# Two of five held chunks become late ones, two sums move one stretch ahead, and a block of the second stage goes first

## The chip, the cores and the metric

The kernel runs on one core of one Trainium2 chip, in float32 throughout. The metric is the device time in microseconds (us) of one execution, median of three runs.

## What is computed

For each of 8 sequences `x` (6400 steps, 128 channels) the kernel computes a causal convolution with a filter `h` as long as the sequence, and then a gated layer on its result:

```
y    = irfft(rfft(x, 2S) * rfft(h, 2S))[:S]          # per channel
gate = sigmoid(sum over k of conv_w[k] * y[t - 4 + k])   # 5 taps, causal
out  = (gate * (y @ w_val)) @ w_out
```

## The kernel before, in words

**Stages.** The transforms are written as matrix products. A sequence is laid out as 100 x 64 (`N1` x `N2`). The **first stage** (`Forward`) takes sums and differences of two halves of `x` (`sums`: one subtraction on GpSimd, POOL in the profile, and one addition, on POOL too inside the main loop) into one of three buffers `sd_0..2`, and multiplies them on TensorE, PE (`half`, 16 small products into two PSUM banks); two copies on ScalarE, ACT, bring the result into `gy`. 16 such blocks make a sequence. The **second stage** (`Product`, 13 blocks `kb`) multiplies `gy` with the constants `m2` on PE; VectorE, DVE, multiplies the result with the filter's spectrum (`mul_u`, `mul_t`), and POOL makes sums of that (`add`), back into `gy`. The constants and the spectrum of each block, 512 KB each, are loaded anew by the queue on SyncE (SP) into slices of one buffer, `ring` (`m2_sb`, `h_sb`). The **third stage** (`s3_quads`, 16 groups) goes from `gy` to `dt`: 64 products on PE, two copies on ACT (`keep`, `ends`) and two joins on DVE (`join`). The **fourth stage** (`s4`) makes the convolved `y` in 13 chunks of 5 (the head: 4) of the 64 columns.

**A chunk's work after `s4`.** ACT copies `y` out of PSUM (`copies`). ACT starts the next columns' gate sums (`init`), and puts the product of one tap into a scratch (`keep`, buffers `keeps`); DVE adds three taps (`taps`, `more`, scalar_tensor_tensor); POOL adds the scratch (`add`). Then PE multiplies `y` with `w_val` (`project`), ACT takes the sigmoid (`sigm`), DVE multiplies (`gate`), PE multiplies with `w_out` (`output`), ACT copies, and SP stores (`store`). Every engine's order is the order of the program text (`_InOrder`), so a waiting instruction holds all that stands behind it on its engine.

**Two stretches per sequence.** In the *third-stage stretch* of sequence b (line 616, group g = 0 to 15) each group holds: third stage of b, one first-stage block of b + 1 with the `sums` for the block two further on, and what `steps[g]` lists: deferred chunk work of b - 1. In the *mixed stretch* (line 665, step s = 0 to 14) stand the fourth stage of b and the second stage of b + 1. So the second stage of b + 1 shares a stretch with the fourth of b, and its products go into `gy` before the next third stage begins.

**Which work is deferred.** `HELD` and `LATE` split the chunks by their first column `a`. Chunks below 10 are done within the mixed stretch. *Held* chunks (10, 15, 20, 25, 30) do their taps and adds in the mixed stretch; projection, gate, output and store wait for groups 0 to 7 of the third-stage stretch. *Late* chunks (35 to 55) have only `y` copied in the mixed stretch; their taps stand two and one groups ahead of their projection. In the mixed stretch the order is head, 0, late ones, 5, held ones, so the held chunks' taps and adds stand at its very end.

**Buffers around the change.** `keeps` has four scratches: two slices of `sd_0` and `sd_1`, and `p_0`, `p_1`. Four single PSUM banks (`single`) go around among `s4`, `half`, `project` and `output`; two pairs (`pair`) among second and third stage. Held gate sums and held `y` lie in `ring`, where `m2_load` and `h_load` of the next sequence may only write once they are out (`AHEAD`). Chunk 5's output is copied into `dt` and stored from there, so the joins of group 0, which write `dt`, wait for that store.

**Where the first two `sums` stand before.** Lines 613 to 615: ahead of group 0, behind the last held chunk's `add` (the `sd` buffers serve as scratches until then). The three loads of `x` they need are issued at step 10 (line 706).

Names in the profile: helpers record every instruction, so all lines read L111; a tile says which work it is: `sd<-x` sums, `pt<-r_sb,sd` first-stage products, `pt<-r_sb,gy` third-stage products, `pt<-gy,ring` second-stage products, `pt<-m_sb,dt` fourth-stage products, `dt<-pt,ring` joins, `gy<-pt,ring` and `ring<-pt,ring 128x1024` the multiplications with the spectrum, SCALAR_TENSOR_TENSOR taps, `pt<-ring,w_sb` and `pt<-yl,w_sb` projections and outputs.

Of the kernel before, what the change touches and what calls it, by code (L numbers as in the profile page):

```python
# [17 lines left out]
N1 = 100  # L18
# [12 lines left out]
CH = 5  # L31
HEAD = (60, 4)
# [2 lines left out]
OUT_ORDER = CHUNKS[1:] + [HEAD]  # L35
LATE = 35
HELD = 10
BL = 2 * SB * C
M2B = 3
MH = 6  # L40
HB = 4
XB = 3
# [81 lines left out]
def longconv_moe(ctx: ExitStack, tc: tile.TileContext, x, h, r1, m2, r3, m4, w64, out):  # L124
    nc = _Engines(tc)
    B = x.shape[0]
# [24 lines left out]
    h_sb = [ring_at[M2B + i] for i in (2, 0, 1, 3)]  # L151
    held_c = ring[:, : (LATE - HELD) * N1].rearrange("p (n t) -> p n t", t=N1)
    held_y = {
        a: ring[:, i : i + CH * N1].rearrange("p (n t) -> p n t", t=N1)
        for a, i in zip(range(HELD, LATE, CH), (2500, 3072, 3572, 4096, 4596))
    }
    x_sb = [cp.tile([128, 2, XG, N2], F32, name=f"x_{i}") for i in range(XB)]
    sd_sb = [cp.tile([128, 2, XG, N2], F32, name=f"sd_{i}") for i in range(3)]
    p_t = [cp.tile([128, CH, N1], F32, name=f"p_{i}") for i in range(2)]
    keeps = [t.rearrange("p a d n -> p (a d n)")[:, : CH * N1].rearrange("p (n t) -> p n t", t=N1) for t in sd_sb[:2]] + p_t  # L160
    hd = dp.tile([NKB, 128, 2 * SB * C], F32, name="hd")

    def weights():
# [66 lines left out]
    def single():  # L230
        return ps1.tile([128, 512], F32, name="pt1", tag="pt1")
# [171 lines left out]
    def cells(x, n):  # L403

        out, i = [], 0
        while i < n:
            y = x + i
            end = next(e for e in (4, HELD, LATE, N2) if y < e)
            k = min(n - i, end - y)
            s = (y - 4) % N2  # L410
            t, o = (gl, y - LATE) if y >= LATE else (held_c, y - HELD) if y >= HELD else (dv[:, :, 1, :N1], s)
            out.append((i, t[:, o : o + k]))
# [3 lines left out]
    class Chunk:  # L416


        def __init__(self, b, i, ch, defer):
            self.b, self.i, self.ch = b, i, ch  # L420
            a, n = ch
            self.late = defer and LATE <= a < HEAD[0]
            self.held = defer and HELD <= a < LATE
            self.y = yl[a][:, :n] if a >= LATE else held_y[a] if a >= HELD else dv[:, a : a + n, 0, :N1]

        def s4(self):
# [39 lines left out]
                self.p = self.y  # L466

        def keep(self):
            self.q = p_t[self.i % 2] if self.late else keeps[self.i % 4]
            self.first(3, self.q, self.p)  # L470

        def init(self):
# [71 lines left out]
    fh, fx = Forward(h, gh, xh), Forward(x[0], gy, xh, NS)  # L544
# [44 lines left out]
    fx = Forward(x[1], gy) if B > 1 else None  # L589
    if fx:  # L590
        fx.load(XB)
    pend = []
    for b in range(B):
        nxt = b + 1 < B


        steps = collections.defaultdict(list)
        for c in pend:
            a = c.ch[0]
            if a == HEAD[0]:  # L600
                t = NS - 1
            elif c.held:
                t = (a - HELD) // CH
            else:
                t = 6 + 2 * (a - LATE) // CH
                steps[t - 2] += [lambda c=c: c.taps(range(2))]
                steps[t - 1] += [lambda c=c: c.taps(range(2, 4)), c.add]
            steps[t] += [c.project, c.sigm, c.gate]
            if t + 2 < NS:
                steps[t + 2] += [c.output]  # L610
                steps[t + 3] += [c.store]
        pend = [c for c in pend if c.ch[0] in (HEAD[0], HEAD[0] - CH)]
        if nxt:
            for _ in range(2):
                fx.sums(nc.gpsimd)
        for g in range(NS):
            e = s3_quads(4 * g)
            f = []
            if nxt:
                f = fx.half([single(), single()])  # L620
                fx.sums(nc.gpsimd)
            for u in e:
                u()
            for u in f:
                u(act)
            if b == 0:
                next(wgen, None)
                next(wgen, None)
                if g % 3 == 0 and g < 12:
                    m4_load(m4_rest.pop(0))  # L630
            if nxt and g in AHEAD:
                f, kb = AHEAD[g]
                (h_load if f else m2_load)(kb)
            for u in steps[g]:
                u()
        if nxt:
            h_load(HB - 1)
        if b + 2 < B:
            fx = Forward(x[b + 2], gy)


        chs = CHUNKS if not nxt else sorted(CHUNKS, key=lambda c: (c != HEAD, c[0] > 0, c[0] < LATE))
        cs = [Chunk(b, i, ch, nxt) for i, ch in enumerate(chs)]
        jobs = collections.defaultdict(list)
        for i, c in enumerate(cs):
            if i and not c.late and not c.held:
                jobs[i + 3].append(c)
        if not nxt:
            jobs[NCH + 2].append(cs[0])
        pr = {}  # L650

        def s2(kb):
            if nxt and kb < NKB:
                pr[kb] = Product(kb)
                m2_load(kb + M2B)

        def times(kb):
            if kb in pr:
                pr[kb].mul_u()
                pr[kb].mul_t()  # L660
                pr.pop(kb).add()
                h_load(kb + HB)

        outs, at = [], 0
        for s in range(max(NCH, *jobs) + 2):
            kbs = list(range(at, min(at + 2 - s % 2, NKB))) if nxt else []
            at += len(kbs)
            if s < 2:
                cs[s].s4()
            late = pend[s : s + 1]  # L670
            if late and s == 0:
                late[0].output()
                late[0].store(p_t[1][:, : HEAD[1]])
                late = []
            if s == 0:
                s2(0)
            for kb in kbs[:1]:
                s2(kb + 1)
            if m4_rest:
                m4_load(m4_rest.pop(0))  # L680
            for c in jobs[s]:
                c.project()
            if 1 < s < NCH:
                cs[s].s4()
            for c in outs + late:
                c.output()
            for c in jobs[s]:
                c.sigm()
            for kb in kbs[:1]:
                times(kb)  # L690
            for kb in kbs[1:]:
                s2(kb + 1)
            if s < NCH:
                cs[s].copies()
            for c in outs + late:
                c.store()
            for kb in kbs[1:]:
                times(kb)
            if 0 < s <= NCH and not cs[s - 1].late:
                cs[s - 1].taps()  # L700
            if 2 < s < NCH + 2 and not cs[s - 2].late:
                cs[s - 2].add()
            for c in jobs[s]:
                c.gate()
            outs = jobs[s]
            if s == 10 and b + 2 < B:
                fx.load(XB)
        pend = [cs[0]] + [c for c in cs if c.held or c.late]


# [43 lines left out]
```

## Time and profile before

| | us |
|---|---|
| three runs, median (lowest to highest) | 1033.85 (1031.86 to 1035.61) |
| profiled execution, its own time | 1034.45 |
| its span | 1032.6 |
| PE busy | 874.2 (85%) |
| DVE busy | 744.7 (72%) |
| POOL busy | 563.4 (55%) |
| ACT busy | 505.1 (49%) |

The granted TensorE clock is 0.953 of full speed in the mean. After a setup the two stretches alternate: the first group of a third-stage stretch starts its first-stage products at 215.24, 337.15, 456.64, 580.04, 699.62 and 818.78 us, so one sequence takes some 120.7 us. The seventh and last third-stage stretch has no next sequence, and no first-stage work.

How to read it: a busy share is a mean over stretches with different limits. A timeline row gives start, length, engine, operation, tiles, count, and in brackets the idle time ahead of it with what ended it. "issue" is idle time for which the profile shows no cause.

### The profile page before, as it was taken

The page shows a single profiled execution, that of the slowest core. Times are in us where ns is not written, and L with a number is a line of the kernel's source. Part 1 is how long each engine was busy: PE and PEld are TensorE (multiplying, and loading weights), DVE is VectorE, ACT ScalarE, POOL GpSimd, SP SyncE. Part 2 cuts the span into 40 slices and gives each one's busy share as a digit, 9 for nine tenths or more (in the row PEclk, how much of TensorE's full clock was granted, in tenths as well). Part 3 has the DMA queues.
Part 4 walks back from the last instruction along what each step waited for, and adds up shares of the span by engine and source line. Part 5 has one row for each costly group of instructions (what it writes and reads, how often), then busy time and mean ns, then how long its engine had stood idle before and what let it go on. Part 6 is the DMA issues. An engine that isn't in the chain of part 4 may idle for free.

```text
span 1032.6 us, 47904 instructions
## 1 busy us (share of the span) xinstructions
PE 874.2 (85%) x21360; PEld 700.7 (68%) x21360; DVE 744.7 (72%) x1049; ACT 505.1 (49%) x1215; POOL 563.4 (55%) x594
## 2 busy tenths in 40 slices
PE   6798679978897979969899698978899698999698
PEld 6798668845696558945588466965579465885464
DVE  5456649758588587867687586984878676888786
ACT  4431542447424673247624484245732575246476
POOL 5457527665386554865357653855648653672122
PEclk9799989989999899989899899998999898999999
DMA  7684649436492466715485355824667154831112
GB/s 245 224 299 182 204 140 329 158 114 187 130 315 75 135 198 210 258 53 165 135 280 180 93 169 167 306 88 129 202 202 268 53 157 149 292 131 53 53 50 98
DMA packets 76364, 177.40 MB, mean 172 GB/s; under 512 B 17792, under 2 KB 29312, under 8 KB 76160
## 3 DMA queue, kind: packets, MB, share of 16 engines
q1 hardware_dynamic: 76160, 174.35, 51.0%
q8 instruction: 168, 2.75, 1.1%
q14 instruction: 36, 0.29, 0.1%
HBM read 141.56 MB, written 32.77 MB: 169 GB/s over the span
## 4 chain that ended last, share of the span: by engine, by line
PE 54%; DVE 12%; issue 9%; ACT 5%; POOL 3%; DMA 1%; DVEq 0%; SPq 0%; ACTq 0%; POOLq 0%
PE pt L111 54%; DVE ring L111 5%; DVE dt L111 4%; DVE gy L111 2%; ACT ring L111 2%; DVE gl L111 2%; DMA ring<-m 1%; POOL gl L111 1%; ACT gl L111 1%; ACT p L111 1%; POOL sd L111 1%; ACT dt L111 1%; POOL ring L111 1%; POOL gy L111 0%; ACT sd L111 0%
## 5 line engine op out<-in xcount | busy, mean ns | idle before, releaser
L111 POOL TENSOR_TENSOR gy<-gy,ring 128x512 f32<-128x512 f32 (+1 forms) x182 | 220.2, 1242 | 122.5 <-DVE ring L111 77.2
L111 PEld LDWEIGHTS pt<-r_sb,gy 64*64 64x64 f32 x8192 | 148.8, 142 | 113.2 <-issue 81.9
L111 POOL TENSOR_TENSOR sd<-x 128x256 f32<-128x256 f32 x236 | 175.4, 770 | 79.7 <-issue 55.3
L111 DVE TENSOR_TENSOR dt<-pt,ring 128x496 f32<-128x496 f32 x256 | 160.1, 667 | 78.7 <-ACT dt L111 78.3
L111 PEld LDWEIGHTS pt<-m_sb,dt 128*64 128x64 f32 x4096 | 185.2, 136 | 39.8 <-issue 11.8
L111 PE MATMUL pt<-r_sb,sd 50*64 50x100 f32 x4608 | 150.9, 270 | 72.2 <-POOL sd L111 42.9
L111 PE MATMUL pt<-m_sb,dt 128*64 128x100 f32 x4096 | 193.8, 249 | 14.5 <-DVE dt L111 6.7
L111 PE MATMUL pt<-r_sb,gy 64*64 64x64 f32 x8192 | 166.2, 230 | 41.4 <-issue 30.0
L111 ACT COPY ring<-pt 128x512 f32<-128x512 f32 (+2 forms) x216 | 129.4, 603 | 145.0 <-PE pt L111 86.7
L111 PE MATMUL pt<-gy,ring 128*64 128x128 f32 x3008 | 188.5, 278 | 12.8 <-PE pt L111 10.3
L111 PEld LDWEIGHTS pt<-gy,ring 128*64 128x64 f32 x3008 | 176.0, 135 | 21.6 <-PE pt L111 17.9
L111 PEld LDWEIGHTS pt<-r_sb,sd 50*64 50x64 f32 x4608 | 126.5, 149 | 79.7 <-POOL sd L111 44.3
L111 DVE TENSOR_TENSOR ring<-pt,ring 128x1024 f32<-128x1024 f32 (+2 forms) x131 | 134.8, 1029 | 51.8 <-PE pt L111 41.4
L111 DVE TENSOR_TENSOR gy<-pt,ring 128x1024 f32<-128x1024 f32 (+1 forms) x99 | 116.8, 1180 | 67.3 <-PE pt L111 63.7
L111 ACT COPY gy<-pt 128x400 f32<-128x400 f32 x248 | 111.3, 504 | 77.8 <-PE pt L111 76.8
L111 POOL TENSOR_TENSOR gl<-gl,p 128x500 f32<-128x500 f32 (+1 forms) x38 | 47.1, 1238 | 143.5 <-DVE gl L111 111.9
L111 ACT COPY dt<-pt 128x16 f32<-128x16 f32 (+3 forms) x317 | 67.4, 265 | 105.0 <-PE pt L111 104.9
L111 ACT COPY yl<-pt 128x500 f32<-128x500 f32 (+1 forms) x89 | 51.1, 574 | 125.0 <-PE pt L111 124.9
L111 DVE SCALAR_TENSOR_TENSOR ring<-pt,w_sb,ring 128x500 f32<-128x500 f32 (+4 forms) x136 | 91.8, 675 | 9.0 <-ACT sd L111 1.7
L111 DVE SCALAR_TENSOR_TENSOR gl<-yl,w_sb,gl 128x500 f32<-128x500 f32 (+1 forms) x112 | 95.6, 858 | 2.8 <-POOL sd L111 1.4
L111 PE MATMUL pt<-ring,w_sb 128*64 128x500 f32 x320 | 84.9, 632 | 1.5 <-DVE ring L111 1.4
L111 DVE TENSOR_TENSOR gl<-pt,gl 128x500 f32<-128x500 f32 (+1 forms) x48 | 31.6, 660 | 34.9 <-ACT gl L111 18.3
(54 smaller groups left out, 751.2 us busy)
## 6 DMA issues: line engine op xcount, KB each, us to landing
ring<-m SPq DMA_DIRECT2D x90, 512.0 KB, 5.2
ring<-hd SPq DMA_DIRECT2D x84, 512.0 KB, 4.7
x<-xl SPq DMA_DIRECT2D x118, 256.0 KB, 3.0
out<-ring SPq DMA_DIRECT2D x40, 250.0 KB, 2.7
out<-yl SPq DMA_DIRECT2D x40, 250.0 KB, 2.7
m_sb<-m SPq DMA_DIRECT2D x12, 375.0 KB, 5.9
hd<-ring SPq DMA_DIRECT2D x8, 512.0 KB, 5.0
out<-dt SPq DMA_DIRECT2D x16, 250.0 KB, 3.8
```

The costliest lines, as they stand in the source:

```text
L111: return self._tc.keep_in_program_order(call(*args, **kwargs))
```

## The change

`WAIT = 25` splits the held chunks: 10, 15 and 20 stay held, 25 and 30 become late ones, with `init`, `keep`, `taps` and `add` in groups 0 to 3 of the third-stage stretch, ahead of their projections, which stay where they were. These taps now read `y` from `ring` instead of PSUM. The scratches no longer use `sd_0` and `sd_1`, but `p_0`, `p_1` and two halves of `h_sb[0]`. That frees `sd_0` and `sd_1`, and the first two `sums` move from the head of the third-stage stretch to steps 9 and 10 of the mixed stretch ahead; the loads of `x` move from step 10 to step 5. Last, the first block of the second stage, `s2(0)`, is issued ahead of the head chunk's `s4`, not behind it.

```diff
+WAIT = 25
...
-    keeps = [t.rearrange("p a d n -> p (a d n)")[:, : CH * N1].rearrange("p (n t) -> p n t", t=N1) for t in sd_sb[:2]] + p_t
+    keeps = p_t + [h_sb[0][:, i : i + CH * N1].rearrange("p (n t) -> p n t", t=N1) for i in (0, BL // 2)]
...
-            self.late = defer and LATE <= a < HEAD[0]
-            self.held = defer and HELD <= a < LATE
+            self.late = defer and WAIT <= a < HEAD[0]
+            self.held = defer and HELD <= a < WAIT
...
-            self.q = p_t[self.i % 2] if self.late else keeps[self.i % 4]
+            self.q = p_t[self.i % 2] if self.late else keeps[(self.i + self.i // 8) % 4]
...
         fx.load(XB)
+        for _ in range(2):
+            fx.sums(nc.gpsimd)
...
-                t = 6 + 2 * (a - LATE) // CH
-                steps[t - 2] += [lambda c=c: c.taps(range(2))]
-                steps[t - 1] += [lambda c=c: c.taps(range(2, 4)), c.add]
+                k = (a - WAIT) // CH
+                t = max(3 + k, 2 + 2 * k)
+                steps[2 * k] += [lambda c=c: c.taps(range(2))]
+                steps[2 * k + 1] += [lambda c=c: c.taps(range(2, 4)), c.add]
...
-        if nxt:
-            for _ in range(2):
-                fx.sums(nc.gpsimd)
...
+            if s == 0:
+                s2(0)
             if s < 2:
                 cs[s].s4()
...
-            if s == 0:
-                s2(0)
...
-            if s == 10 and b + 2 < B:
-                fx.load(XB)
+            if b + 2 < B:
+                if s == 5:
+                    fx.load(XB)
+                if s in (9, 10):
+                    fx.sums(nc.gpsimd)
```

**POOL, end of the mixed stretch and start of the third-stage stretch**, before: the last second-stage `add`, then the chunks' adds (their target is `dt`, `ring` or `gl`), then the sums.

```order
L111 TENSOR_TENSOR gy<-gy,ring 128x64x4 x2
L111 TENSOR_TENSOR dt<-dt,p_88 128x2x100
L111 TENSOR_TENSOR ring<-ring,p_88 128x300
L111 TENSOR_TENSOR ring<-ring,sd_84 128x500
L111 TENSOR_TENSOR ring<-ring,sd_85 128x500
L111 TENSOR_TENSOR ring<-ring,p_87 128x500
L111 TENSOR_TENSOR ring<-ring,p_88 128x500
L111 TENSOR_TENSOR ring<-ring,sd_84 128x200
L111 TENSOR_TENSOR gl<-gl,sd_84 128x300
L111 TENSOR_TENSOR sd_84<-x_81 128x256 x2
L111 TENSOR_TENSOR sd_85<-x_82 128x256 x2
L111 TENSOR_TENSOR sd_86<-x_83 128x256 x2
```

The same place now (a scratch in `h_sb[0]` shows as `ring`):

```order
L112 TENSOR_TENSOR gy<-gy,ring 128x64x4 x2
L112 TENSOR_TENSOR dt<-dt,ring 128x2x100
L112 TENSOR_TENSOR ring<-ring 128x300
L112 TENSOR_TENSOR sd_84<-x_81 128x256 x2
L112 TENSOR_TENSOR ring<-ring,p_88 128x500
L112 TENSOR_TENSOR sd_85<-x_82 128x256 x2
L112 TENSOR_TENSOR ring<-ring 128x500 x2
L112 TENSOR_TENSOR sd_86<-x_83 128x256 x2
L112 TENSOR_TENSOR sd_84<-x_81 128x256 x2
L112 TENSOR_TENSOR ring<-ring,p_88 128x500
L112 TENSOR_TENSOR sd_85<-x_82 128x256 x2
```

The first two pairs of sums now stand behind the adds of chunks 5 and 10; chunk 25's add stands behind two further pairs, inside group 1.

**DVE at the same border**, before: taps of chunk 30, then the joins of group 0 (`dt<-pt,ring`), a gate (`ring<-pt,ring`), the next joins.

```order
L111 SCALAR_TENSOR_TENSOR ring<-pt_2955,w_sb,ring 128x500
L111 SCALAR_TENSOR_TENSOR ring<-pt_2955,w_sb,ring 128x400
L111 SCALAR_TENSOR_TENSOR gl<-pt_2955,w_sb,gl 128x100
L111 SCALAR_TENSOR_TENSOR ring<-pt_2955,w_sb,ring 128x300
L111 SCALAR_TENSOR_TENSOR gl<-pt_2955,w_sb,gl 128x200
L111 TENSOR_TENSOR dt<-pt_2998,ring 128x124x4
L111 TENSOR_TENSOR dt<-pt_2998,ring 128x62x2x4
L111 TENSOR_TENSOR ring<-pt_3059,ring 128x500
L111 TENSOR_TENSOR dt<-pt_3064,ring 128x124x4
L111 TENSOR_TENSOR dt<-pt_3064,ring 128x62x2x4
L111 TENSOR_TENSOR ring<-pt_3125,ring 128x500
```

Now, from the taps of chunk 20 on:

```order
L112 SCALAR_TENSOR_TENSOR ring<-pt_2895,w_sb,ring 128x500 x3
L112 TENSOR_TENSOR dt<-pt_2982,ring 128x124x4
L112 TENSOR_TENSOR dt<-pt_2982,ring 128x62x2x4
L112 TENSOR_TENSOR ring<-pt_3043,ring 128x500
L112 SCALAR_TENSOR_TENSOR ring<-ring,w_sb 128x500 x2
L112 TENSOR_TENSOR dt<-pt_3052,ring 128x124x4
L112 TENSOR_TENSOR dt<-pt_3052,ring 128x62x2x4
L112 TENSOR_TENSOR ring<-pt_3113,ring 128x500
L112 SCALAR_TENSOR_TENSOR ring<-ring,w_sb 128x500
L112 TENSOR_TENSOR dt<-pt_3120,ring 128x124x4
L112 TENSOR_TENSOR dt<-pt_3120,ring 128x62x2x4
```

The joins of group 0 follow chunk 20's taps, and chunk 25's taps stand behind the gates of groups 0 and 1; chunk 30's follow in groups 2 and 3.

**PE at the border the other way**, from the third-stage into the mixed stretch, before: the head chunk's projection for sequence b - 1, the head chunk's `s4` for b, the head chunk's output for b - 1, and the first two blocks of the second stage for b + 1.

```order
L111 MATMUL pt_4095<-yl_74,w_sb 64x400 x2
L111 MATMUL pt_4103<-m_sb,dt 64x2x50 x16
L111 MATMUL pt_4120<-gl,w_sb 64x400 x2
L111 MATMUL pt_4125<-gy,ring 64x64x2 x16
L111 MATMUL pt_4143<-gy,ring 64x64x2 x16
```

Now:

```order
L112 MATMUL pt_4095<-yl_74,w_sb 64x400 x2
L112 MATMUL pt_4103<-gy,ring 64x64x2 x16
L112 MATMUL pt_4121<-m_sb,dt 64x2x50 x16
L112 MATMUL pt_4138<-gl,w_sb 64x400 x2
L112 MATMUL pt_4143<-gy,ring 64x64x2 x16
```

The first second-stage block has changed places with `s4` and the output. On SP, two loads of `x` that each wait for one of the moved pairs of sums now stand ahead of chunk 5's store from `dt`; before they stood behind it.

## The prediction

> **What bounds the kernel now.** I read the page first. PE is the busiest engine and heads the chain that ended last, so what PE waits for comes next.
>
> ```profile
> PE 54%; DVE 12%; issue 9%; ACT 5%; POOL 3%; DMA 1%; DVEq 0%; SPq 0%; ACTq 0%; POOLq 0%
> ```
>
> The waits: one PE wait is long and rare, six times up to 7.2 us for the first-stage sums; the other has no cause in the profile.
>
> ```profile
> PE pt L111 <- issue: 50.8, 34, 4.2
> ...
> PE pt L111 <- POOL sd L111: 42.9, 6, 7.2
> ```
>
> Six is the number of third-stage stretches that carry first-stage work and follow a mixed stretch. PE's timeline at one of these borders (start, length, tiles, count):
>
> ```profile
> 448.30 1.19 PE L111 MATMUL pt<-r_sb,gy 64*64 64x64 f32 x64
> 456.64 1.61 PE L111 MATMUL pt<-r_sb,sd 50*64 50x100 f32 x32 [7.16 <-POOL sd L111]
> ...
> 461.57 0.86 PE L111 MATMUL pt<-r_sb,sd 50*64 50x100 f32 x32
> ...
> 463.36 1.19 PE L111 MATMUL pt<-r_sb,gy 64*64 64x64 f32 x64
> 464.37 0.87 PE L111 MATMUL pt<-r_sb,sd 50*64 50x100 f32 x32
> ...
> 467.00 1.19 PE L111 MATMUL pt<-r_sb,gy 64*64 64x64 f32 x64
> ```
>
> Group 0's third-stage products end at 449.5, and its first-stage block starts at 456.64. After the wait the same work also takes longer: 1.61 against 0.86 us for a block. The view by stretches says why: the granted clock (the third figure from the end) is 0.50 behind the wait, and 1.00 from the next block on.
>
> ```profile
> 456.70:460.00 3.30, 3.30 (x36) 1.54 (x36) 0.00 (x0) 1.41 (x3) 2.62 (x4) 0.50 0.50 153
> 461.60:467.00 5.40, 5.40 (x153) 3.02 (x143) 3.19 (x5) 4.15 (x12) 2.81 (x5) 1.00 0.51 162
> ```
>
> POOL in the time of the wait, in the order of its text:
>
> ```profile
> 452.53 1.24 POOL L111 TENSOR_TENSOR ring<-ring,p 128x500 f32<-128x500 f32 x1 [1.00 <-issue]
> 453.73 0.60 POOL L111 TENSOR_TENSOR ring<-ring,sd 128x200 f32<-128x200 f32 x1
> ...
> 455.19 4.14 POOL L111 TENSOR_TENSOR sd<-x 128x256 f32<-128x256 f32 x6
> ```
>
> The sums stand behind chunk 30's add (at 453.73 the first of its two pieces), and that behind chunk 30's taps on DVE, the second of these rows:
>
> ```profile
> 445.45 4.70 DVE L111 SCALAR_TENSOR_TENSOR ring<-pt,w_sb,ring 128x500 f32<-128x500 f32 x6
> ...
> 450.32 1.41 DVE L111 SCALAR_TENSOR_TENSOR ring<-pt,w_sb,ring 128x500 f32<-128x500 f32 x2 [0.17 <-ACT sd L111]
> ```
>
> **Part 1: the first sums move ahead.** The first pair of sums now stands behind chunk 5's add and the second behind chunk 10's, so neither waits for chunks 15 to 30. Chunk 20's taps are the first three of the six at 445.45, over at 447.8; chunk 10's lie ahead of 445.45. So both pairs are there before 449.5, and group 0's first-stage block can follow its third-stage products at once. Its first PSUM bank is chunk 20's, free at 447.8 as well. This removes the wait, 42.9 us in all, and the slow start behind it: block to block it is 461.57 - 456.64 = 4.93 us after the wait, 464.37 - 461.57 = 2.80 in the next group, which has the same projection and third-stage work. That is 2.13 us here; at another border
>
> ```profile
> 215.24 1.61 PE L111 MATMUL pt<-r_sb,sd 50*64 50x100 f32 x32 [7.15 <-POOL sd L111]
> ...
> 219.76 0.86 PE L111 MATMUL pt<-r_sb,sd 50*64 50x100 f32 x32
> ```
>
> it is 4.52 - 2.80 = 1.72. Taking 1.9, six times: 11.5 (10.3 to 12.8). Part 1 gains 42.9 + 11.5 = 54.4 us.
>
> The same slow start by a page: the Trainium skill, TensorE: Matmul & The Clock Gate, Part 1 (the HAM clock gate), halves PE's clock after an idle window of about 3.4 us until one such window of work has passed; an estimate by its figure is 1.7 us for each wait, 53.1 instead of 54.4 in all. By that rule the clock at 0.50 behind the wait is as it should be, and the rows differ from the estimate by 0.2 us a wait.
>
> What is late next? Group 0's joins on DVE. They follow chunk 20's taps, so DVE is free for them at 447.8 and their PSUM is ready about 450.1. But they write `dt`, so they wait for chunk 5's store out of it:
>
> ```profile
> 447.30 0.55 SPq L111 DMA_DIRECT2D out<-dt  x1
> ```
> ```profile
> out<-dt SPq DMA_DIRECT2D x16, 250.0 KB, 3.8
> ```
>
> On SP this store now stands behind a load of `x` that waits for the second pair of sums, which I place at some 447.7; so it issues at about 448.1, and lands at 451.9. The joins then end at 453.2, and PE's group 2, which needs their PSUM pair, comes about 454: just hidden, by 0.9 us.
>
> **Part 2: taps of chunks 25 and 30 move.** PE's work in each group is the same as before. On DVE about 5.2 us leave the mixed stretch, where it has no slack, for groups 0 to 3:
>
> ```profile
> L111 DVE TENSOR_TENSOR dt<-pt,ring 128x496 f32<-128x496 f32 x256 | 160.1, 667 | 78.7 <-ACT dt L111 78.3
> ...
> L111 DVE SCALAR_TENSOR_TENSOR gl<-yl,w_sb,gl 128x500 f32<-128x500 f32 x105 | 89.5, 852 | 2.8 <-POOL sd L111 1.4 <-ACT gl L111 0.2
> ...
> L111 DVE SCALAR_TENSOR_TENSOR ring<-pt,w_sb,ring 128x500 f32<-128x500 f32 x104 | 76.7, 738 | 8.7 <-ACT sd L111 1.7 <-ACT p L111 1.5 <-DVE ring L111 0.5
> ...
> L111 POOL TENSOR_TENSOR sd<-x 128x256 f32<-128x256 f32 x236 | 175.4, 770 | 79.7 <-issue 55.3 <-PE pt L111 13.6 <-DMA x<-hl 4.7
> ...
> L111 DVE TENSOR_TENSOR ring<-pt,ring 128x500 f32<-128x500 f32 x40 | 27.0, 676 | 45.3 <-PE pt L111 41.4 <-ACT ring L111 3.2
> ```
>
> Six taps at 852 ns, the price with `y` from SBUF (738 from PSUM), are 5.1; two are cut in two pieces, so 5.2. With eight joins at 667 (5.3) and four gates at 676 (2.7) DVE has 13.2 us to do in groups 0 to 3. PE needs 467.00 - 463.36 = 3.64 for a group with projection and output, 14.6 for four. So it fits, at 90%, with little room: a late gate or sigmoid then shows. The nearest row for such a chain is in the last stretch, where ACT waits for POOL's add:
>
> ```profile
> 963.35 0.62 ACT L111 ACTIVATE gl<-gl 128x500 f32<-128x500 f32 x1 [2.45 <-POOL gl L111]
> ```
>
> I bound what comes back by 0 and 2.5 us a sequence and take 1.0, nearer to nothing since PE hides most of it: 6 x 1.0 = 6.0. ACT's four moved activations and POOL's two adds stand in groups where those engines have idle time.
>
> The seventh stretch has no first-stage work, so DVE sets its pace already:
>
> ```profile
> 955.43 1.20 PE L111 MATMUL pt<-r_sb,gy 64*64 64x64 f32 x64 [0.95 <-DVE dt L111]
> ...
> 961.43 1.19 PE L111 MATMUL pt<-r_sb,gy 64*64 64x64 f32 x64 [0.79 <-DVE dt L111]
> ```
>
> There the 5.2 us are only moved, but the two new chains through ACT and POOL may add waits: 1.0 us (0 to 4).
>
> **Part 3: second stage's first block first.** At the other border:
>
> ```profile
> 391.83 0.89 PE L111 MATMUL pt<-yl,w_sb 128*64 128x400 f32 x4
> 393.51 1.69 PE L111 MATMUL pt<-m_sb,dt 128*64 128x100 f32 x31 [0.78 <-DVE dt L111]
> ...
> 395.66 4.00 PE L111 MATMUL pt<-gy,ring 128*64 128x128 f32 x64
> 400.43 2.07 PE L111 MATMUL pt<-gy,ring 128*64 128x128 f32 x32 [0.78 <-PE pt L111]
> ```
> ```profile
> 391.97 0.90 ACT L111 COPY gy<-pt 128x400 f32<-128x400 f32 x2
> ```
> ```profile
> 397.84 1.22 DVE L111 TENSOR_TENSOR gy<-pt,ring 128x1024 f32<-128x1024 f32 x1 [3.94 <-PE pt L111]
> ...
> 400.24 1.22 DVE L111 TENSOR_TENSOR gy<-pt,ring 128x1024 f32<-128x1024 f32 x1
> ```
>
> `s2(0)` needs only `gy`, complete at 392.9, where `s4` waited for the joins until 393.5. The four pieces to the end of `s2(1)` took 393.51 to 399.66; started at 392.9 they end at 399.1. DVE has then done block 0's two products and starts block 1's at 399.2 instead of 400.24. From there DVE runs without a gap and PE waits for it, so 1.0 us is gained at each of 7 borders: 7.0. It is 0 if PE sets the pace there, and 1.6 (both waits of 0.78) at most.
>
> **The sum.** 1034.45 - 54.4 - 7.0 + 6.0 + 1.0 = 980.05. The median of the runs lies 0.6 below the profiled execution: **979**. With all bounds on one side: 1034.45 - 55.7 - 11.2 - 0.6 = 967, and 1034.45 - 53.2 + 15 + 4 - 0.6 = 1000.
>
> **The rivals.**
>
> *DVE and POOL in each other's way (1008).* The moved taps read two SBUF operands while POOL makes sums. The Trainium skill, SBUF — State Buffer, "SBUF: two separate sides", speaks against the move: DVE with two SBUF inputs and a POOL operation exclude each other for a whole instruction. As a mechanism of this kernel: eight pieces, each held by one of POOL's sums (770 ns), are 6.2 us more, so DVE has 19.4 us in groups 0 to 3 against PE's 14.6; 4.8 us come back in six sequences, 979 + 29. For it: 852 against 738 ns. Against it: that is 0.11, not 0.77 a piece. 13%.
>
> *The first block still waits (1027).* If something else of group 0 or the chunks ahead ends as late as the sums did, only part 3 is left: 1034.45 - 7.0 - 0.6. The profile names no such wait: the PSUM bank and the adds ahead are free by 447.8. 6%.
>
> *Slower: PE starves for instructions (1050).* PE waits 50.8 us with no cause in the profile, in pieces such as
>
> ```profile
> 490.47 0.40 PE L111 MATMUL pt<-r_sb,gy 64*64 64x64 f32 x10 [2.35 <-issue]
> ```
>
> which lies in the middle of a third-stage group, where no product waits for another engine, while the loads for the second stage run. If the 7 us rests were what lets PE's supply catch up, new pieces of 2.35 + 1.9 us (slow start) would take their place. With 2.4 of them a sequence all is lost; with three, 6 x 12.8 = 76.5, and the sum is 1034.45 - 54.4 - 7.0 + 76.5 + 1.0 = 1050. Against it: PE is busy for all 5.40 us from 461.6 to 467.0, so the supply keeps up for a while at least. 5%.
>
> **Chances.** The forecast with its bounds has 76%, the rivals in their order 13, 6 and 5. The range reaches down to 965 and up past the first rival to 1010, since my bounds are from few rows. A measurement of this kernel can tell about 0.3% (3 us) from no change. The forecast and the first rival are faster, the second half of the time (if part 3 gives less it is the same): faster 0.92, same 0.03, slower 0.05.
>
> **What would show it.** Right: no PE wait for `sd` at the six borders, a first block of 0.87 us, the third-stage groups 0 to 3 at 3 to 3.7 us, a period near 112 us, block 1's products on DVE some 1 us earlier. Wrong: joins of group 0 that wait for `out<-dt` past 453; DVE without a gap in groups 0 to 3 with PE waiting for `dt`; more "issue" than 50.8 us.

## The result and the profile after

| | before | after |
|---|---|---|
| median of four runs (lowest to highest), us | 1032.93 (1031.86 to 1035.61) | 983.71 (982.08 to 984.52) |
| profiled execution, its own time | 1034.45 | 983.02 |
| its span | 1032.6 | 980.9 |
| PE / DVE / POOL / ACT busy | 85 / 72 / 55 / 49% | 88 / 76 / 59 / 52% |
| granted TensorE clock, mean | 0.953 | 0.979 |

The ratio is 0.9518, 95% interval 0.9494 to 0.9542. 979.0 was forecast, in a range of 965 to 1010. In the sets of runs below, single executions in a slower state of the chip are left out (of the changed kernel's second set one, at 997.09 us).

The chain that ended last has the same head; POOL's share of it went from 3 to 1%:

```profile
PE 52%; DVE 13%; issue 8%; ACT 5%; DMA 4%; POOL 1%; SPq 0%; DVEq 0%; ACTq 0%; POOLq 0%
```

The waits (total us, times, longest). PE's row for the sums, 42.9 us before, is gone. PE's short waits for DVE are about as long in all as they were, 32.1 us against 31.1, with more of them for `ring`. New is a row of DVE's, for a store. Before:

```profile
PE pt L111 <- DVE dt L111: 20.9, 22, 2.4
...
PE pt L111 <- DVE ring L111: 10.2, 24, 1.4
```

After:

```profile
PE pt L112 <- issue: 53.1, 39, 3.1
...
DVE dt L112 <- DMA out<-dt: 18.2, 4, 5.1
PE pt L112 <- DVE dt L112: 16.6, 17, 2.3
PE pt L112 <- DVE ring L112: 15.5, 32, 1.4
```

PE's timeline after at the border that the prediction showed (group 0 then at 448.30, its first-stage block at 456.64):

```profile
430.16 1.19 PE L112 MATMUL pt<-r_sb,gy 64*64 64x64 f32 x64
431.17 0.87 PE L112 MATMUL pt<-r_sb,sd 50*64 50x100 f32 x32
431.97 1.06 PE L112 MATMUL pt<-ring,w_sb 128*64 128x500 f32 x4
432.95 1.21 PE L112 MATMUL pt<-r_sb,gy 64*64 64x64 f32 x64
...
439.31 1.06 PE L112 MATMUL pt<-ring,w_sb 128*64 128x500 f32 x4 [0.68 <-DVE ring L112]
```

The block follows group 0's products at once and takes 0.87 us; the clock (third figure from the end) is full from the first group on, where it was 0.50 behind the wait:

```profile
430.20:451.00 20.80, 19.26 (x610) 12.12 (x608) 16.52 (x26) 16.67 (x45) 13.98 (x17) 1.00 0.42 117
```

DVE's timeline there. The first row is chunk 20's taps; then 4.66 us of nothing, then joins, gates and taps end to end:

```profile
427.31 2.28 DVE L112 SCALAR_TENSOR_TENSOR ring<-pt,w_sb,ring 128x500 f32<-128x500 f32 x3
434.25 1.25 DVE L112 TENSOR_TENSOR dt<-pt,ring 128x496 f32<-128x496 f32 x2 [4.66 <-PE pt L112]
435.42 0.67 DVE L112 TENSOR_TENSOR ring<-pt,ring 128x500 f32<-128x500 f32 x1
436.00 1.51 DVE L112 SCALAR_TENSOR_TENSOR ring<-ring,w_sb 128x500 f32<-128x500 f32 x2
...
441.57 1.98 DVE L112 SCALAR_TENSOR_TENSOR ring<-ring,w_sb 128x500 f32<-128x500 f32 x2
...
450.33 0.66 DVE L112 TENSOR_TENSOR ring<-pt,ring 128x500 f32<-128x500 f32 x1
```

POOL there: chunk 25's add at 440.05 has waited for its taps, and behind it come sums again.

```profile
432.16 2.81 POOL L112 TENSOR_TENSOR sd<-x 128x256 f32<-128x256 f32 x4
440.05 1.26 POOL L112 TENSOR_TENSOR ring<-ring,p 128x500 f32<-128x500 f32 x1 [5.08 <-DVE ring L112]
441.27 1.86 POOL L112 TENSOR_TENSOR sd<-x 128x256 f32<-128x256 f32 x2
```

SP's queue explains DVE's 4.66 us, for which the row names PE: chunk 5's store out of `dt` was issued at 430.04, behind two loads of `x`, and landed at 434.06.

```profile
426.70 3.24 SPq L112 DMA_DIRECT2D x<-xl  x2
430.04 0.55 SPq L112 DMA_DIRECT2D out<-dt  x1
```

At the other border, PE and DVE after. The second stage's first block comes 1.08 us behind the start of the head's projection, and `s4` behind it:

```profile
374.98 0.89 PE L112 MATMUL pt<-yl,w_sb 128*64 128x400 f32 x4
376.06 2.07 PE L112 MATMUL pt<-gy,ring 128*64 128x128 f32 x32 [0.19 <-ACT gy L112]
377.96 1.55 PE L112 MATMUL pt<-m_sb,dt 128*64 128x100 f32 x32
```
```profile
382.09 1.23 DVE L112 TENSOR_TENSOR gy<-pt,ring 128x1024 f32<-128x1024 f32 x1 [1.41 <-PE pt L112]
```

Block 1's products start on DVE 382.09 - 374.98 = 7.11 us behind the projection; before it was 400.24 - 391.83 = 8.41.

Where the time went, by PE's timeline (means of six sequences): a third-stage stretch, from group 0 to the head's projection, took 64.28 us and takes 56.32; a mixed stretch, from there to the next group 0, took 56.37 and takes 55.29. 6 x (7.96 + 1.08) = 54.2 us. The last stretch went from 44.44 to 45.59, what follows the last projection from 57.32 to 58.78, and the first sequence's two stretches from 52.56 + 54.59 to 54.39 + 53.42; with 0.67 us less in the setup that makes 51.6, and the span fell by 51.7. (The first sequence's two stretches together take 107.2 to 109.3 us in the 14 profiles, so its 0.66 us more say nothing about the change.)

### The profile page after: what moved, and what is told of

Read it like the earlier page. It is cut to its first block, busy times and chain, and to the rows that moved or that the text cites. A ratio compares the mean times of both kernels' runs of the same rounds, so it can differ in the third digit from the quotient of the medians.

```text
span 980.9 us, 47924 instructions
## 1 busy us (share of the span) xinstructions
PE 861.9 (88%) x21360; PEld 695.4 (71%) x21360; DVE 749.7 (76%) x1049; ACT 507.6 (52%) x1215; POOL 574.1 (59%) x594
## 4 chain that ended last, share of the span: by engine, by line
PE 52%; DVE 13%; issue 8%; ACT 5%; DMA 4%; POOL 1%; SPq 0%; DVEq 0%; ACTq 0%; POOLq 0%
PE pt L112 52%; DVE ring L112 6%; DVE dt L112 4%; DMA ring<-m 3%; ACT ring L112 3%; DVE gl L112 2%; DVE gy L112 1%; POOL gl L112 1%; ACT gy L112 1%; ACT dt L112 1%; DMA out<-dt 0%; ACT p L112 0%; ACT yl L112 0%; POOL ring L112 0%; ACT gl L112 0%
## 5 line engine op out<-in xcount | busy, mean ns | idle before, releaser
L112 POOL TENSOR_TENSOR sd<-x 128x256 f32<-128x256 f32 x236 | 185.4, 815 | 31.4 <-issue 19.7
L112 PE MATMUL pt<-r_sb,sd 50*64 50x100 f32 x4608 | 148.0, 263 | 30.4 <-issue 20.9
L112 PEld LDWEIGHTS pt<-r_sb,sd 50*64 50x64 f32 x4608 | 123.7, 144 | 37.9 <-issue 26.7
L112 DVE TENSOR_TENSOR ring<-pt,ring 128x1024 f32<-128x1024 f32 (+2 forms) x131 | 134.4, 1026 | 6.7 <-ACT ring L112 0.2
L112 POOL TENSOR_TENSOR gl<-gl,p 128x500 f32<-128x500 f32 (+1 forms) x45 | 53.2, 1184 | 110.8 <-DVE gl L112 89.2
L112 DVE SCALAR_TENSOR_TENSOR gl<-yl,w_sb,gl 128x500 f32<-128x500 f32 (+1 forms) x112 | 99.5, 893 | 2.1
L112 PE MATMUL pt<-ring,w_sb 128*64 128x500 f32 x320 | 80.1, 598 | 8.9 <-DVE ring L112 8.8
L112 DVE SCALAR_TENSOR_TENSOR ring<-pt,w_sb,ring 128x500 f32<-128x500 f32 (+3 forms) x94 | 63.1, 671 | 6.1 <-ACT ring L112 1.5
L112 POOL TENSOR_TENSOR ring<-ring,p 128x500 f32<-128x500 f32 (+1 forms) x23 | 24.7, 1074 | 60.7 <-DVE ring L112 44.1
```

The lines of the kernel that those rows point to most:

```text
L112: return self._tc.keep_in_program_order(call(*args, **kwargs))
```

## The experiments

Each ratio is to the kernel before, run on the same chip, with its 95% interval; us by ratio are of 1032.9. Medians of one kernel in two sets of runs can differ by some 5 us, as the changed kernel's second set shows, so the ratios are the better guide.

### Each part alone, and the whole less one part

**s2(0) back at its old place.** The changed kernel with

```
             if s < 2:
                 cs[s].s4()
...
+            if s == 0:
+                s2(0)
             for kb in kbs[:1]:
```

> The changed kernel with s2(0) back behind the head chunk's s4 (part 3 undone). The prediction's theory: the first second-stage block at its new place saves 1.0 us at each of seven borders into the mixed stretch, so this takes 983.7 + 7 = 990.7 us, 988.5 to 993, and the mixed stretches (head projection to next third-stage group 0) are 56.2 to 56.4 us again instead of 55.2. Rival: the 1.08 us that the mixed stretch lost came from the 5.2 us of taps that left its end, and s2's place gives nothing: 983.7, 982 to 986, with mixed stretches of 55.2 to 55.4.

Measured: 995.55 us (992.66 to 1002.2), 0.9626 (0.9577 to 0.9677), 994 by ratio. The mixed stretches are 56.44 in the mean, as expected. So part 3's 1.1 us a border are its own and not the moved taps'. That is 1 to 3 us above the expected range. The profile, of the slowest of the four runs (1002.2 us), has the excess in groups 7 to 15 of the third-stage stretch: from group 7 to the head's projection it takes 32.2 us in the mean, where the changed kernel took 30.7, with 36.0 us of PE's waits without a cause there against 31.4. Up to group 7 the two agree within 0.2 us. Why this run had more of these waits isn't settled.

**s2(0) first, alone.** The kernel before with the same block moved up.

> The kernel before with s2(0) ahead of the head chunk's s4 and nothing else. The prediction's theory: DVE paces the mixed stretch and starts block 1's products 1.0 us earlier at each of seven borders, so 1032.9 - 7 = 1026, 1023.5 to 1028; the 7.16 us waits for the sums stay as they are. Rival: at the end of the mixed stretch something else is then late (the adds on POOL, which still end in front of the sums), and the gain comes back as a longer wait for the sums: 1032.9, 1031 to 1034.

Measured: 1028.93 us (1026.16 to 1033.32), 0.9936 (0.9908 to 0.9964), 1026.3 by ratio. The mixed stretches are 55.20, and PE's wait for the sums is unchanged (43.0 us, 6 times). The theory holds.

**The sums ahead, alone.** The kernel before with `keeps`, the loads of `x` and the two `sums` as in the change, and `WAIT = 35`, so that no held chunk becomes a late one.

> The kernel before with only the first sums (their loads and the scratches with them) moved into the stretch ahead; chunks 25 and 30 stay held and s2(0) stays behind s4. The prediction's theory: the place of the sums on POOL makes the wait. The 7.16 us and the slow clock go; left are about 0.7 us for chunk 25's bank (its taps end at 450.2, group 0's third-stage products at 449.5) and about 1.3 us for block 2's sums, which stand behind chunk 30's add. So 9.07 - 2.0 = 7.1 us come off each of six third-stage stretches: 1032.9 - 42 = 991, 985 to 998. Rival: the five held chunks at the end of the mixed stretch are what binds (chunk 30's taps on DVE stand ahead of the joins, chunk 30's add ahead of block 2's sums), and without their move PE waits again one or two groups later for as long: 1015 to 1033.

Measured: 990.94 us (990.51 to 991.91), 0.9574 (0.9539 to 0.9609), 988.9 by ratio. The rival falls: without any move of taps the 42.9 us go, but for 3.8 us of waits for a later pair of sums.

**The late chunks, alone.** The kernel before with `WAIT = 25` and the new `steps`; `keeps`, `sums` and loads as they were.

> The kernel before with only chunks 25 and 30 made late ones; the first sums stay at the head of the third-stage stretch and s2(0) stays behind s4. The prediction's theory: the sums then stand behind chunk 20's add, 450 instead of 453.7 to 454.4, so the first two pairs end near 451.8 and not at 456.6: a wait of 2 to 3 us instead of 7.16 is left at each of six borders, and less of the slow clock behind it. Gain 5 to 7 us a border less 1.0 for the moved taps: 1032.9 - 6 x 5.3 + 1 = 1002, 995 to 1008. If it comes with the sums alone to more than the two together gain, the two edits take the same wait. Rival: the sums were late by their own length (three pairs, 4.6 us of POOL) and not by what stands ahead of them, so the wait stays over 5 us: 1020 to 1033.

Measured: 1006.28 us (997.37 to 1008.46), 0.9705 (0.9647 to 0.9762), 1002.4 by ratio. PE's timeline at the border, and its clock:

```profile
436.35 1.19 PE L112 MATMUL pt<-r_sb,gy 64*64 64x64 f32 x64
439.79 1.20 PE L112 MATMUL pt<-r_sb,sd 50*64 50x100 f32 x32 [2.25 <-POOL sd L112]
440.92 1.94 PE L112 MATMUL pt<-ring,w_sb 128*64 128x500 f32 x4
```
```profile
439.80:443.10 3.30, 3.30 (x48) 1.49 (x52) 0.71 (x3) 2.06 (x5) 2.67 (x4) 0.57 0.52 140
```

A wait of 2.25 us is left, and the slow clock behind it. Alone the two edits gain 4.3 and 3.0%, and the first run above, which has both, 3.7: they take the same wait.

**All but part 2.** The run with the sums alone, and `s2(0)` first.

```
+            if s == 0:
+                s2(0)
             if s < 2:
                 cs[s].s4()
```

> The kernel before with the sums moved ahead and s2(0) first, but with all five held chunks still done in the mixed stretch: the whole change but for part 2. The prediction took part 2 as needed for the gain (it gives back 1.0 us a sequence, and without it 2.0 us of the wait stay), so by it this is slower than the changed kernel: 983.7 - 7 + 12 = 989, 986 to 993. Rival: the move of chunks 25 and 30 is worth nothing, as the run with the sums alone (0.9574) and the one with s2(0) alone (0.9936) already add up to the whole change: 0.9574 - 0.0064 = 0.951 of the time before, the same as the changed kernel within 3 us.

Measured: 981.27 us (977.32 to 989.62), 0.9498 (0.9454 to 0.9541), the same as the whole change within the intervals. The rival holds: the move of chunks 25 and 30 is worth nothing that these runs, with some 0.5% of noise, can tell. DVE and PE at the border show why:

```profile
436.74 1.41 DVE L112 SCALAR_TENSOR_TENSOR ring<-pt,w_sb,ring 128x500 f32<-128x500 f32 x2 [0.17 <-ACT p L112]
438.07 0.31 DVE L112 SCALAR_TENSOR_TENSOR gl<-pt,w_sb,gl 128x100 f32<-128x100 f32 x1
438.30 0.52 DVE L112 SCALAR_TENSOR_TENSOR ring<-pt,w_sb,ring 128x300 f32<-128x300 f32 x1
438.74 0.42 DVE L112 SCALAR_TENSOR_TENSOR gl<-pt,w_sb,gl 128x200 f32<-128x200 f32 x1
439.07 1.25 DVE L112 TENSOR_TENSOR dt<-pt,ring 128x496 f32<-128x496 f32 x2
...
443.11 1.25 DVE L112 TENSOR_TENSOR dt<-pt,ring 128x496 f32<-128x496 f32 x2 [0.46 <-ACT dt L112]
```
```profile
434.72 1.19 PE L112 MATMUL pt<-r_sb,gy 64*64 64x64 f32 x64
...
439.21 0.91 PE L112 MATMUL pt<-r_sb,sd 50*64 50x100 f32 x30 [0.24 <-DVE gl L112]
...
442.99 0.92 PE L112 MATMUL pt<-r_sb,sd 50*64 50x100 f32 x32 [0.76 <-POOL sd L112]
```

The taps of 25 and 30 run behind PE's last fourth-stage products, so they lengthen no mixed stretch (55.11 us, against 55.29 in the changed kernel). They hold the joins of group 0 until 439.07, 4.35 us behind group 0; in the changed kernel the store holds them until 4.09. PE loses 0.24 and 0.76 us, and then DVE has gaps while PE works, 4.6 to 4.9 us of them up to the joins of group 4. Group 7 begins 25.0 to 26.6 us behind group 0 here and 25.4 to 25.9 in the changed kernel.

### Does DVE set the pace of groups 0 to 3?

The changed kernel with four additions on DVE more in each of groups 0 to 3 of the six stretches.

```
+    junk = cp.tile([128, CH * N1 // 2], F32, name="junk")
+    nc.vector.memset(junk, 0.0)
...
             for u in steps[g]:
                 u()
+            if b and nxt and g < 4:
+                for _ in range(4):
+                    nc.vector.tensor_tensor(out=junk, in0=junk, in1=junk, op=ADD)
```

> The changed kernel with 16 additions of 250 columns on DVE, which compute nothing that is used, added to groups 0 to 3 of the six third-stage stretches with first-stage work, four behind each group's own work: some 6 to 7 us of DVE (0.40 us each, an estimate between 0.68 us for 500 columns and nothing). Theory: DVE sets the pace of these groups in the changed kernel (no gap from 434.25 to 451), so nearly all of it comes back: 983.7 + 6 x 6 = 1020, 1010 to 1026. The prediction's cover of 1.4 us by PE would leave 4.6 to 5.6 a sequence, 1011 to 1017. Rival: DVE's lag is made up in groups 8 to 15, where it has gaps of 1 to 1.7 us: under 1000.

Measured: 1043.56 us (1040.66 to 1049.45), 1.0104 (1.0054 to 1.0153). The additions took longer than estimated:

```profile
L112 DVE TENSOR_TENSOR junk<-junk 128x250 f32<-128x250 f32 x96 | 61.1, 636 | 2.5
```

61.1 us more on DVE, and (1.0104 - 0.9518) x 1032.9 = 60.5 us more in the time: one for one. That is beyond the expected 1010 to 1026, but by the size of the additions, not by the theory. From the first join of group 0 to the first of group 4 DVE took 12.47 us in the changed kernel, with 0.07 us of gaps, and takes 21.7 here, with 0.5. DVE sets the pace of these groups and PE covers nothing. The timelines of DVE and POOL in two of its groups show one thing more, which bears on the first rival:

```profile
462.41 1.77 DVE L112 TENSOR_TENSOR junk<-junk 128x250 f32<-128x250 f32 x4
...
466.50 3.52 DVE L112 TENSOR_TENSOR junk<-junk 128x250 f32<-128x250 f32 x4
```
```profile
466.73 1.28 POOL L112 TENSOR_TENSOR ring<-ring,p 128x500 f32<-128x500 f32 x1 [6.97 <-DVE ring L112]
467.97 2.63 POOL L112 TENSOR_TENSOR sd<-x 128x256 f32<-128x256 f32 x3
```

Four additions take 1.77 us while POOL stands still and 3.52 while it adds. The single instructions in the trace show how. Of the second four the first, begun 0.23 us ahead of POOL's addition, takes 0.41 us like those beside a still POOL. The second begins at 466.94, within POOL's addition, takes 1.34 us and ends 0.28 us behind it; the next two end as far behind a POOL sum each. So it is with all 42 additions of this run that begin while a POOL instruction runs: each ends 0.27 to 0.28 us behind that instruction's end. The moved taps show the same. In the changed kernel the eight pieces of a sequence take 5.86 us in each of the six stretches with sums, and 4.82 in the last one, where POOL makes none: three of the eight begin beside POOL's sums and lose 1.0 us together. Taps with an operand in PSUM lose nothing: a piece of 500 columns takes 0.74 us in the kernel before, beside POOL or not.

### The store out of `dt`

**A first try,** with chunk 5's output put into the first half of `h_sb[0]` (`keeps[2]`). It overwrites chunk 15's scratch, so one tap of chunk 15 is not the reference's.

```
-                c.store()
+                c.store(keeps[2] if nxt and c.ch[0] == CH else None)
```

> The changed kernel with chunk 5's output copied into and stored from a scratch (the first half of h_sb[0], free by then) and not out of dt, so that the joins of group 0 wait for no store. In the changed kernel these joins start at 434.25, 4.1 us behind group 0's first product, and DVE then works without a gap up to 451 while PE waits for it a few times, 3.8 us in all. Theory A: that lateness of DVE is what makes groups 2 to 7 slow (group 7 begins 25.6 us behind group 0, where PE alone needs 2.8 + 2.8 + 5 x 3.64 = 23.8). Without the store the joins start 1.8 to 2.2 us earlier and up to 1.8 us come off each of six stretches: 973 to 980. Rival: groups 8 to 15, with PE's waits without a cause, take back what groups 0 to 7 gain: group 7 comes earlier and the time stays at 982 to 985.

Measured: 978.71 us (973.97 to 983.78), 0.9455 (0.9415 to 0.9495).

**The same with `p_0`,** which is free then, beside the changed kernel run again on the same chip.

```
-                c.store()
+                c.store(p_t[0] if nxt and c.ch[0] == CH else None)
```

> The changed kernel with chunk 5's output copied into and stored from p_0, which is free at that time, and not out of dt. The run with the first half of h_sb[0] overwrote chunk 15's tap there, so its output was not the reference's; this one computes the reference. Theory: as in that run, the joins of group 0 start some 2 us earlier, group 7 begins 24.3 us behind group 0 and not 25.6, and it takes 0.6% less than the changed kernel: 976 to 980 us, a ratio near 0.946. Rival: the gain was noise between two sets of runs (0.9455 against 0.9518, with intervals that touch), or came from the changed data, and this takes the time of the changed kernel.

> The changed kernel itself once more, for comparison on the same chip with the three others. 0.9518 of the time before, 982 to 985 us, if this chip is like the first; its place against the store out of p_0 says what that store costs.

Measured: 978.66 us (976.15 to 982.75), 0.9472 (0.9436 to 0.9509), against 988.63 (982.2 to 990.92), 0.9541 (0.9492 to 0.9589), for the changed kernel: 0.7% less by the ratios. The intervals still touch, the two sets of runs hardly do. PE and DVE at the border with the store out of `p_0`:

```profile
428.71 1.19 PE L112 MATMUL pt<-r_sb,gy 64*64 64x64 f32 x64
429.72 0.87 PE L112 MATMUL pt<-r_sb,sd 50*64 50x100 f32 x32
430.52 1.06 PE L112 MATMUL pt<-ring,w_sb 128*64 128x500 f32 x4
```
```profile
430.74 1.25 DVE L112 TENSOR_TENSOR dt<-pt,ring 128x496 f32<-128x496 f32 x2 [2.60 <-ACT dt L112]
```

The joins start 2.03 us behind group 0, not 4.09, and wait for ACT's copy alone. In the first three of the six sequences group 7 then begins 24.3 to 24.8 us behind group 0, against 25.4 to 25.9; in the other three PE lost 0.9 to 1.4 us in groups 1 and 2 to waits without a cause, and group 7 begins 25.3 to 26.8 us behind. In the mean of the six that is 25.2 us, against 25.6 and 25.8 in the two profiles of the changed kernel, so the profiles place 3 to 4 us of the gain here and leave some of it open. Part 2's own price shows in group 5: it takes 4.1 us in those first three sequences, for DVE, and 3.1 to 3.3 in the kernel before and with all but part 2. The last stretch shows the store most cleanly, since nothing else moves there: 45.36 to 45.59 us in the seven profiles with the late chunks and the store out of `dt`, 44.75 in each of the three with the late chunks and the store from elsewhere, 44.44 to 44.55 in the four with all five chunks held. Of part 2's 1.0 us there, some 0.7 is the store and 0.3 the taps.

### PE's waits without a cause

**Loads spread out.** The changed kernel with

```
-AHEAD = {2: (1, 0), 7: (0, 0), 9: (0, 1), 10: (0, 2), 11: (1, 1), 13: (1, 2)}
+AHEAD = {2: (1, 0), 5: (0, 0), 7: (0, 1), 9: (0, 2), 11: (1, 1), 13: (1, 2)}
```

> The changed kernel with the loads of the second stage's constants and spectra put into groups 2, 5, 7, 9, 11, 13 of the third-stage stretch, not 2, 7, 9, 10, 11, 13, so that fewer loads of 512 KB run at once. Theory: PE's waits without a cause in groups 8 to 15 (53.1 us in all, up to 3.1 us at a time) are its instructions arriving late behind these loads; with the loads spread the waits fall by a third or more and the third-stage stretches get 1 to 3 us shorter: 966 to 978. Rival: the waits have nothing to do with when these loads are issued: 53 us of them stay within 6 us, and 981 to 986.

Measured: 992.58 us (990.44 to 1000.85), 0.9614 (0.9573 to 0.9655). Neither: PE's wait for "issue" rose to 65.7 us, and the time is 1% above the changed kernel's. Spreading the loads is no cure. Why the wait rose isn't settled.

**Fewer loads.** The six loads only in the first sequence's stretch, so six stretches are without them.

```
-            if nxt and g in AHEAD:
+            if nxt and g in AHEAD and b == 0:
```

> The changed kernel without the six loads of 512 KB in the third-stage stretch from the second sequence on (the second stage then computes with old data, so the output is not the reference's). Theory: PE's waits without a cause in groups 8 to 15 come when its instructions arrive late behind these loads, so without them 53.1 us of such waits fall to 20 to 30 us, and five stretches get 3 to 6 us shorter each: 955 to 970 us. Rival: the waits belong to the instruction supply itself or to what the profile does not record, and stay at 45 to 55 us: 978 to 985.

Measured: 970.77 us (969.52 to 972.32), 0.9391 (0.9351 to 0.9431), at the upper end of what was expected. The waits of PE with fewer loads, and those of the changed kernel on the same chip:

```profile
PE pt L112 <- issue: 38.7, 33, 3.9
```
```profile
PE pt L112 <- issue: 52.9, 40, 3.2
```

The total, 38.7 us, fell less far than the expected 20 to 30, but it hides the place. Summed over PE's timeline from 26 us behind group 0 to the head's projection, in six stretches, "issue" is 14.7 us with fewer loads, and 29 to 33 in the kernel before, the changed one (both runs), the sums alone, all but part 2 and the store out of `p_0`. 15.6 us of the rest lie in the first sequence, which keeps its loads. From group 7 to the head's projection a stretch takes 28.5 us in the mean without the loads, at a clock of 1.00, and 31.3 at 0.96 in the changed kernel run again. The third of the six, the changed kernel's longest, without the loads and with them:

```profile
453.20:481.10 27.90, 24.84 (x880) 17.59 (x872) 24.09 (x34) 20.78 (x60) 15.76 (x18) 1.00 0.32 98
```
```profile
459.10:492.50 33.40, 27.78 (x896) 20.91 (x888) 23.66 (x34) 21.11 (x58) 15.48 (x18) 0.85 0.52 159
```
```profile
467.78 0.39 PE L112 MATMUL pt<-r_sb,gy 64*64 64x64 f32 x10 [2.36 <-issue]
...
483.21 1.01 PE L112 MATMUL pt<-r_sb,gy 64*64 64x64 f32 x27 [2.71 <-issue]
```

27.9 against 33.4 us, at a clock of 1.00 against 0.85. That the loads make about half of these waits is shown; that what comes late is PE's instructions fits, but no run shows it, and what makes the other half is open.

**Loads later,** with the store out of `p_0`.

```
-AHEAD = {2: (1, 0), 7: (0, 0), 9: (0, 1), 10: (0, 2), 11: (1, 1), 13: (1, 2)}
+AHEAD = {2: (1, 0), 8: (0, 0), 10: (0, 1), 12: (0, 2), 13: (1, 1), 14: (1, 2)}
```

> The store out of p_0 and, on top of it, the loads of the third-stage stretch in groups 2, 8, 10, 12, 13, 14 and not 2, 7, 9, 10, 11, 13. Loads moved ahead to groups 5, 7, 9 had cost 9 us. Theory: a load that is issued while SP still has loads of x and stores for groups 5 to 9 to issue delays these, so later ones help: 2 to 6 us less than the store out of p_0 alone, 970 to 976. Rival: the waits without a cause move with the loads and their number stays: 976 to 981; or the second stage's first blocks wait for their data: over 985.

Measured: 981.86 us (973.97 to 983.24), 0.9486 (0.9446 to 0.9526): no gain over the store out of `p_0` alone, with 57.8 us of "issue" against 59.9. The rival holds: the waits move with the loads. Against the changed kernel those of group 9 fall from 7.0 to 0.6 us in six stretches, and those of group 14 rise from 4.8 to 15.9.

Of the versions that compute the reference, the changed kernel with the store out of `p_0` has the lowest ratio, 0.9472. All but part 2 comes to 0.9498, which the intervals don't tell from it.

## Why the prediction was right, and where it was not

**Part 1, the sums: right.** The six waits and the slow blocks behind them are gone, the first block takes the 0.87 us, and the sums alone bring 4.3%. But not all of the 9.07 us a border arrived at once. Before, group 7 began 32.5 to 33.1 us behind group 0, and 9.07 less would be 23.7; it is 25.4 to 25.9. Two of the nine us were lost on the way.

**"Just hidden, by 0.9 us": the first step that failed.** The joins of group 0 do wait for chunk 5's store, to 4.09 us behind group 0, close to the 3.6 forecast, and PE's group 2 does start on time (435.77, 5.6 behind group 0). What I left out is what stands behind the joins on DVE: a gate and two taps in each group, all 2 us late with them. PE meets that lateness at the end of group 2 (the row at 439.31). By the order of the text that is chunk 20's projection, and it waits 0.68 us for chunk 15's gate, which frees a PSUM bank. The store out of `p_0` gave back 0.7% of the time.

**Part 2, "fits at 90%": the second step that failed.** PE's side of that sum was too large. The 3.64 us hold for groups with a projection and an output, and outputs begin in group 2; groups 0 and 1 take 2.80, as the prediction's own row for group 1 says. So PE needs 2 x 2.80 + 2 x 3.64 = 12.9 us and not 14.6, which is what the first three sequences with the store out of `p_0` take (12.88). Against that, 13.2 us on DVE are 103%, and the 12.47 measured are 97%. With its start at 4.09 on top, DVE has no cover in groups 0 to 3: 61.1 us of further work on it cost 60.5. DVE's work was sized well; PE's was not, and DVE's start was not in the sum. Nor did the taps lengthen the mixed stretch, as the prediction had it. And the part brought nothing that the sums ahead had not: where the chunks stay held, their taps end at the same 4 us behind group 0 and then leave DVE idle. I priced what the move costs (1.0 us a sequence) and never asked what the change would be without it. The net of parts 1 and 2 came out right, 7.96 us a sequence against 8.07, since a loss of two by group 7 was set against one forecast, and 0.8 us came back behind group 7. That is luck. PE's waits there sum to 33 us before and 35 after, but the clock behind them differs: from group 7 to the head's projection a stretch took 31.5 us at a mean clock of 0.94 before, 30.7 at 0.98 in the changed kernel, and 31.3 at 0.96 in its second profile. No part of the change aims there, and single sequences of one kernel differ by more (55.56 to 57.20 in the changed one).

**Part 3: right.** 1.08 us a border in six mixed stretches and 1.17 in the first, against 1.0, by the mechanism named: undone, it goes; alone, it comes.

**The last stretch:** 1.15 us against 1.0. The 1.46 us behind the last projection were not forecast and belong to no part: this tail takes from 57.09 to 60.23 us in the 14 profiled kernels, whether they have a part or not.

**The rivals.** *The first block still waits*: no. *DVE and POOL in each other's way*: the mechanism is there, its price was not. The rival charged each of eight pieces a whole sum, 6.2 us; the moved taps lost 1.0 us a sequence, since five of the eight begin while POOL rests and the others part-way into one of its instructions. The Trainium skill, SBUF — State Buffer, "SBUF: two separate sides", has the two exclude each other for a whole instruction. The trace agrees: each of the 42 additions that began within a POOL instruction ended 0.27 to 0.28 us behind it. *PE starves for instructions*: "issue" grew by 2.3 us, not by 70. The waits are real and come in part from the loads, but the 7 us rests were not what kept them down: in groups 8 to 15 they are 29 us before and 31 after.

Of the prediction's signs of being wrong, DVE without a gap in groups 0 to 3 showed, with PE waiting for gates and not for `dt`, and so did more "issue" than 50.8 us (53.1). The time came out inside the range all the same, with part 1 and part 3 carrying it.

## What to carry to other kernels

When two edits in one change aim at the same wait, price each without the other: here the sums alone bring it all, and moving taps from one place into the next, where DVE has no room either, brings nothing. When something is "just hidden", follow the late engine to the end of its queue, not only to the first consumer: 2 us of lateness in front of a queue that is 97% full stays. When two engines are compared over several groups, add up what each group holds: here the first two had no output, and 1.7 of PE's 14.6 us were never there. A buffer that is stored from and written next is a wait in the making; here a free scratch took it away.

## What the runs showed of the hardware

- A PE wait well under the 7 us of before can cost the clock too. Behind 2.25 us (the late chunks alone) it was 0.57 for the next 3.3 us, and in the changed kernel's second profile two waits of 2.36 and 2.71 us stand in a stretch at 0.85. It need not: over the 14 profiles, from 105 us on, of PE's waits that began at full clock, the next 3.3 us were below 0.9 behind 1 of 212 that lasted 1 to 1.5 us, 40 of 70 of 2 to 2.5 us, 20 of 23 of 3 to 3.5 us, and all 21 above that. The Trainium skill, TensorE: Matmul & The Clock Gate, Part 1 (the HAM clock gate), names an idle window of about 3.4 us; many of these waits are shorter and still cost the clock, so the measurements go below that rule.
- An addition on DVE with both operands in SBUF takes twice as long in the mean while POOL adds (0.88 against 0.44 us for 250 columns), because it ends 0.27 to 0.28 us behind the POOL instruction within which it began. A tap with an operand in PSUM isn't held (0.74 us either way).
- Loads of 512 KB hold up PE with no cause in the profile: without six of them in each stretch its "issue" waits in groups 8 to 15 fall from 31 to 14.7 us.
- The changed kernel's runs spread by 8.8 us (982.1 to 990.9 over both sets), more than the 3 us that the prediction gave to a measurement.
